# Two small groups of attention matmuls issued as pairs on halves of the TensorE array

## The chip, the cores and the metric

The kernel runs on one core of one Trainium2 chip. The metric is the device time of one execution in microseconds (us). Three runs of the kernel before gave 1731.4, 1724.58 and 1718.41 us; the median is 1724.58 us.

## The reference

Inputs: q, k, v of shape 8 x 8 x 576 x 64 (batch, heads, sequence, head size), p of shape 8 x 8 x 32 x 64, and the weights of two feed-forward blocks. All are float32.

```python
def sm_attn(qq, kk, vv):
    s = scale * np.matmul(qq, kk.transpose(0, 1, 3, 2))
    a = np.exp(s - np.max(s, axis=-1, keepdims=True))
    a = a / (np.sum(a, axis=-1, keepdims=True) + 1e-09)
    return np.matmul(a, vv)
p_packed = sm_attn(p, k, v)
x = sm_attn(q, p_packed, p_packed)          # 4608 x 512 once heads are side by side
xn = x / sqrt(mean(x * x, -1) + 1e-06) * rms_g
y = (silu(xn @ w_gate) * (xn @ w_val)) @ w_out     # inner width 1536
h = y @ w_in                                        # inner width 2048
out = np.maximum(0.01 * h, h) @ w_out2
```

The two feed-forward blocks are nearly all of the arithmetic. The attention's second output is never formed for them: `A` (the second softmax's weights) is kept, the packed values are multiplied into `w_gate` and `w_val` (tile `pw`), and `x` itself is only needed for its mean of squares.

## The kernel before, in words

Attention is done in 16 units, one for a batch and half of its heads (four heads, `u` = 0 or 1). A unit has two parts. `soft1` (lines 224 to 389) does the first softmax. Its function `packed` (line 332) makes `Pm`, the packed values of four heads as a block diagonal 128 x 256: the weights `a1T` lie 96 rows by 128 columns (four heads of 32 columns each), the values `vr` 96 rows by 256 columns (four heads of 64), and six products add up in one PSUM bank `pp`. Every head's columns of weights meet every head's values, so 128 x 256 results come out of which the four diagonal blocks of 32 x 64 are wanted; the product with `mask` on VectorE (line 344) sets the rest to zero. These products are plain float32, and the profile shows each as two passes: 96 products, 192 rows of PE.

`soft2` (line 393) does the second softmax. Its function `squares` (line 505) forms `x` for the four heads, 256 columns by 576 tokens, in four products `xp`: `x` = 0 or 1 picks two heads (two heads' `Pm` as stationary operand, 128 rows by 128 columns, of which the rows of the other two heads are zero) and `c` a half of 288 tokens. ScalarE squares what is in PSUM (line 539) and GpSimd adds the squares up (line 543, from batch 2 on); for units 0 to 5 the products are plain float32 (line 532), for units 6 to 15 each is three single-pass products of float32r halves (`mm3`, line 113: high by high, low by high, high by low). `means` (line 545) sums over the columns with a product by ones.

The rest of the PE work is `mm3` as well: `pwps` (weights times packed values), `g` and `v`, `y`, and for the second block `zh`/`h` and `zo`/`o`. Units 0 to 7 lie in the first 320 us, beside the start of the first feed-forward block; units 8 to 15 lie in a stretch from about 530 to 890 us, woven into the second block on the first half of the tokens (`zh`, `zo`).

What sets the order: the tables `S1`, `S2`, `FIRST`, `SECOND` give each function a slot in the recorded program; a list scheduler with a time model of its own then moves single instructions of each engine, taking into account when their inputs and PSUM banks come free. PE, VectorE, ScalarE, GpSimd and SyncE (the DMA queue) each run their own list in order. PSUM banks for `pp` and `xp` come from the four `y` banks (`bank`, line 205; `banks`, line 194); in the first units, from the `g` and `v` banks.

Of the kernel before, what the change touches and what calls it, by code (L numbers as in the profile page):

```python
# [30 lines left out]
FASTQ = 6  # L31
# [9 lines left out]
def pack_attention_moe_kernel(  # L41
# [14 lines left out]
    nc = tc.nc  # L56
# [6 lines left out]
    P = 128  # L63
    T = 32
    NS = S // T
    CS = NS // 2
    CH = CS * T
    KP = 96
    NJ = S // KP
# [37 lines left out]
    def mm3(ps, terms, start=True, stop=True):  # L107
        seq = [t for hi, lo in (("h", "h"), ("l", "h"), ("h", "l")) for t in [(hi, lo)]]
        n = len(terms) * 3
        i = 0  # L110
        for a, b in seq:
            for (lh, ll), (rh, rl) in terms:
                mm = nc.tensor.matmul(  # L113
                    ps,
                    lhsT=lh if a == "h" else ll,
                    rhs=rh if b == "h" else rl,
                    start=start and i == 0,
                    stop=stop and i == n - 1,
                )
                i += 1  # L120
        return mm
# [104 lines left out]
    def soft1(i):  # L226
# [105 lines left out]
        def packed():  # L332
            vr = raw.pop(("v", b, u))
            pp = bank("pp" + nm)
            for j in range(NJ):
                nc.tensor.matmul(  # L336
                    pp[:, 0, :256],
                    lhsT=st["a1T"][:, j // 3, j % 3, :],
                    rhs=vr[:, :, j, :],
                    start=j == 0,  # L340
                    stop=j == NJ - 1,
                )
            Pm = st["Pm"] = att.tile([P, 4, D], F32, tag="Pm", bufs=2, name="Pm" + nm)
            nc.vector.scalar_tensor_tensor(
                out=Pm.rearrange("p h d -> p (h d)"),
                in0=pp[:, 0, :256],
                scalar=st["rin"],
                in1=mask.rearrange("p h d -> p (h d)"),
                op0=ALU.mult,
                op1=ALU.mult,  # L350
            )
            if i + 1 < NU and i + 1 != NA:
                load_v(*divmod(i + 1, 2))
# [39 lines left out]
    def soft2(i):  # L393
# [6 lines left out]
        def tile_of(key, tag, shape):  # L400
            if key not in st:
                st[key] = att.tile(shape, F32, tag=tag, bufs=bufs[tag], name=key + nm)
            return st[key]
# [98 lines left out]
                ]  # L502
                split(AT.rearrange("p s t -> p (s t)"), *st["ATs"])

        def squares(cs, x):
            Pm = raw["P", b, u][0]
            first = u == 0 and x == 0
            early = b < SUMS
            if early:

                if first:
                    sqacc[b] = []
                if u == 0:
                    if x == 0:
                        st["sq"] = keep.tile([P, 2, 2, CH], F32, tag="atf", bufs=1, name="sq" + nm)
                    sq = st["sq"][:, x]
                else:
                    sq = att.tile([P, 2, CH], F32, tag=("sq", "sql")[x], bufs=1, name=f"sq{x}" + nm)
                sqacc[b].append(sq)
            elif first:  # L520
                sq = sqacc[b] = tile_of("sqa", "sqacc", [P, 2, CH])
            else:
                sq = att.tile([P, 2, CH], F32, tag="sq", bufs=1, name=f"sq{x}" + nm)
            for xp, cs in banks(f"xp{x}" + nm, b):
                for k_, c in enumerate(cs):
                    if i >= FASTQ:
                        ds, ts = slice(x * P, x * P + P), slice(c * CH, c * CH + CH)
                        ph, pl = st["Pm"]
                        ah, al = st["ATs"]
                        mm3(xp[:, k_, :CH], [((ph[:, ds], pl[:, ds]), (ah[:, ts], al[:, ts]))])  # L530
                        continue
                    nc.tensor.matmul(
                        xp[:, k_, :CH],
                        lhsT=Pm[:, 2 * x : 2 * x + 2, :].rearrange("p h d -> p (h d)"),
                        rhs=st["AT"][:, c * CS : (c + 1) * CS, :],
                        start=True,
                        stop=True,
                    )
                nc.scalar.activation(
                    out=sq[:, cs[0] : cs[-1] + 1], in_=xp[:, :, :CH], func=AF.Square  # L540
                )
            if not first and not early:
                side[0].tensor_tensor(out=sqacc[b], in0=sqacc[b], in1=sq, op=ALU.add)

        def means(cs):
            parts = sqacc[b]
# [851 lines left out]
```

## Time and profile before

| | before |
|---|---|
| runs, us | 1718.41, 1724.58, 1731.4 (median 1724.58) |
| span of the profiled execution, us | 1725.8 |
| PE busy | 1660.3 us, 96% of the span, 9252 instructions |
| weight loads busy | 1468.4 us, 85% |
| VectorE busy | 971.7 us, 56% |
| ScalarE busy | 693.5 us, 40% |
| GpSimd busy | 396.3 us, 23% |
| mean granted clock of TensorE | 0.986 of full speed |

The profiled execution's own time is known by its span, 1725.8 us, which is 1.2 us over the median of the three runs. A matmul's row in the trace begins when it enters the array and ends when its last result is written, so neighbours overlap; what one costs in a full stream is the distance between two starts, which I call the cadence.

### The profile page before, as it was taken

Reading aid. Unit: us, or ns where it says so; the run is one execution under the profiler, and the core shown is the slowest. Engines: PE = TensorE matmul, PEld = TensorE weight load, DVE = VectorE, ACT = ScalarE, POOL = GpSimd, SP = SyncE. Lnnn points to the kernel's source line nnn. Section 1 sums busy time; section 2 is a strip of 40 time slices with the busy share of each in tenths; the row PEclk is TensorE's granted clock in tenths of the full one; section 3 lists DMA queues with packets and bytes.
Section 4 is the critical chain, followed back from the end, with each engine's and each line's share of the span. In section 5 each row is a group of like instructions: output and inputs, shape, how many; then the busy total and the mean of one; then the engine's idle time right before and its main releaser. Section 6 shows DMA issues by size and latency. Waiting matters only on the chain.

```text
span 1725.8 us, 23867 instructions
## 1 busy us (share of the span) xinstructions
PE 1660.3 (96%) x9252; PEld 1468.4 (85%) x9252; DVE 971.7 (56%) x1636; ACT 693.5 (40%) x1218; POOL 396.3 (23%) x310
## 2 busy tenths in 40 slices
PE   7698989999999999999999999999999999999997
PEld 5587889999998888888888999999988888888885
DVE  6877887788757777666644455545542323232221
ACT  3465554564425554444434433444322223222221
POOL 2355555533311232221221112322100000000000
PEclk9889999999999999999999999999999999999998
DMA  9856666587646554642317332634063101010000
GB/s 291 235 193 189 209 205 192 191 304 260 239 152 234 181 195 146 217 156 77 101 53 267 109 122 98 233 140 155 32 245 127 49 1 48 2 46 4 18 8 25
DMA packets 83365, 247.98 MB, mean 144 GB/s; under 512 B 11444, under 2 KB 17844, under 8 KB 79156
## 3 DMA queue, kind: packets, MB, share of 16 engines
q1 hardware_dynamic: 80052, 235.96, 40.1%
q0 software_dynamic: 3200, 10.49, 2.5%
q8 instruction: 73, 1.20, 0.3%
q14 instruction: 40, 0.33, 0.1%
HBM read 174.85 MB, written 61.08 MB: 137 GB/s over the span
## 4 chain that ended last, share of the span: by engine, by line
PE 79%; DMA 9%; DVE 6%; issue 2%; ACT 2%; POOL 1%; SPq 0%; DVEq 0%; ACTq 0%; POOLq 0%
PE y L113 13%; PE h L113 13%; PE o L113 13%; PE zh L113 9%; PE zo L113 9%; PE v L113 7%; PE g L113 7%; PE pwps L113 3%; PE pp L336 2%; DMA pw<-w 2%; PE s L113 1%; DMA q<-in_q_dram 1%; DMA w<-in_moe_w_in_dram 1%; DVE cvw L692 1%; PE xp L113 1%
## 5 line engine op out<-in xcount | busy, mean ns | idle before, releaser
L113 PE MATMUL y<-hh,wo 128*128 128x288 f32 x1536 | 269.2, 298 | 4.7 <-DVE y_acc L913 2.4
L113 PEld LDWEIGHTS y<-hh,wo 128*128 128x128 f32 x1536 | 226.5, 189 | 8.0 <-DVE y_acc L913 2.7
L138 POOL TENSOR_TENSOR hl<-sg,hh 128x576 fp32r<-128x576 f32 x96 | 140.8, 1467 | 349.5 <-ACT hh L130 335.5
L113 PE MATMUL o<-w,gh 128*128 128x512 f32 x640 | 212.5, 392 | 0.0
L913 DVE TENSOR_TENSOR y_acc<-y_acc,y 128x288 f32<-128x288 f32 x320 | 142.1, 450 | 104.9 <-PE y L113 103.6
L1310 DVE TENSOR_TENSOR gf<-r,h 128x512 f32<-128x512 f32 x80 | 55.0, 688 | 248.6 <-ACT r L130 248.6
L113 PE MATMUL zo<-w,zgh 128*128 128x512 f32 x512 | 172.7, 394 | 0.0
L113 PE MATMUL y<-hl,wo 128*128 128x288 f32 x768 | 164.0, 297 | 0.0
L113 PE MATMUL h<-yh,w 128*128 128x512 f32 x640 | 162.5, 393 | 0.5 <-DVE y_acc L913 0.5
L113 PE MATMUL zh<-zyh,w 128*128 128x512 f32 x512 | 161.1, 392 | 1.7 <-DVE y_acc L913 1.7
L130 ACT ACTIVATE r<-h 128x512 f32<-128x512 f32 x80 | 47.8, 598 | 261.0 <-PE h L113 261.0
L113 PE MATMUL g<-ath,pw 128*128 128x288 f32 x768 | 141.8, 299 | 8.4 <-DMA pw<-w 6.4
L113 PEld LDWEIGHTS h<-yh,w 128*128 128x128 f32 x640 | 120.0, 188 | 28.1 <-DVE y_acc L913 0.8
L113 PEld LDWEIGHTS o<-w,gh 128*128 128x128 f32 x640 | 120.1, 188 | 27.1
L138 DVE TENSOR_TENSOR pw<-pwps,pw 64x512 fp32r<-64x512 f32 x152 | 104.1, 688 | 63.0 <-ACT pw L130 60.4
L113 PE MATMUL v<-ath,pw 128*128 128x288 f32 x768 | 138.5, 299 | 0.7 <-DVE sg L890 0.6
L130 ACT ACTIVATE hh<-sg 128x576 fp32r<-128x576 f32 x96 | 65.6, 683 | 164.8 <-DVE sg L890 160.3
L113 PEld LDWEIGHTS g<-ath,pw 128*128 128x128 f32 x768 | 117.6, 189 | 15.8 <-issue 6.1
L113 PE MATMUL o<-w,gl 128*128 128x512 f32 x320 | 125.0, 391 | 0.0
L113 PEld LDWEIGHTS y<-hl,wo 128*128 128x128 f32 x768 | 124.3, 190 | 0.1
L113 PEld LDWEIGHTS v<-ath,pw 128*128 128x128 f32 x768 | 115.7, 191 | 2.1 <-DVE sg L890 1.4
L890 DVE TENSOR_TENSOR sg<-sg,v 128x576 f32<-128x576 f32 x96 | 72.2, 752 | 72.1 <-PE v L113 66.1
(161 smaller groups left out, 3072.6 us busy)
## 6 DMA issues: line engine op xcount, KB each, us to landing
w<-w_dram SPq DMA_DIRECT2D x72, 512.0 KB
w<-w_dram SPq DMA_DIRECT2D x32, 1024.0 KB
wo<-wo_dram SPq DMA_DIRECT2D x36, 512.0 KB
w_dram<-w2s SPq DMA_DIRECT2D x32, 512.0 KB
w_dram<-w SPq DMA_DIRECT2D x24, 512.0 KB
pw<-w POOLq DMA_DIRECT2D x40, 256.0 KB, 5.4
y_dram<-y_acc SPq DMA_DIRECT2D x32, 288.0 KB
w<-in_moe_w_in_dram SPq DMA_DIRECT2D x16, 512.0 KB
```

The costliest lines, as they stand in the source:

```text
L113: mm = nc.tensor.matmul(ps, lhsT=lh if a == "h" else ll, rhs=rh if b == "h" else rl, start=start and i == 0, stop=stop and i == n - 1,)
L130: nc.scalar.activation(out=o, in_=i, func=AF.Copy, scale=scale)
L138: eng.tensor_tensor(out=o, in0=a, in1=hi.bitcast(F32), op=ALU.subtract)
L336: nc.tensor.matmul(pp[:, 0, :256], lhsT=st["a1T"][:, j // 3, j % 3, :], rhs=vr[:, :, j, :], start=j == 0, stop=j == NJ - 1,)
L692: nc.vector.scalar_tensor_tensor(out=cu, in0=low, scalar=29, in1=cu, op0=ALU.logical_shift_right, op1=ALU.bitwise_or,)
L890: nc.vector.tensor_tensor(out=hf, in0=sg, in1=vps[:, :, :CH], op=ALU.mult)
L913: pace[:] = [nc.vector.tensor_tensor(out=ya, in0=ya, in1=pv, op=ALU.add).ins]
L1310: pace[:] = [nc.vector.tensor_tensor(out=gf, in0=r, in1=ps, op=ALU.max).ins]
```

## The change

In `packed`, each of the six products becomes two: one with columns 0 to 63 of the weights (heads 0 and 1 of the unit) and their own 128 columns of values, one with columns 64 to 127 and the other two heads' values. The first writes PSUM partitions 0 to 63, the second 64 to 127, both the same 128 columns of one bank. They are given to the two halves of the array's columns (tiles of 128 rows x 64 columns). VectorE's masking reads the 128 columns twice, for 256 results as before.

In `squares`, `x` = 0 needs only rows 0 to 63 of the operands and `x` = 1 only rows 64 to 127, since the other rows of `Pm` are zero there. Each product now reads only its 64 rows, on the matching half of the array's rows (tiles of 64 rows x 128 columns). The function is called per half of the tokens (`c`) and not per `x`; within a call the products of the two `x` alternate, each `x` in a PSUM bank of its own. The number of `xp` products stays. ScalarE squares each bank alone; GpSimd's adds are cut differently, with one more per unit where `u` is 1.

```diff
             for j in range(NJ):
-                nc.tensor.matmul(
-                    pp[:, 0, :256],
-                    lhsT=st["a1T"][:, j // 3, j % 3, :],
-                    rhs=vr[:, :, j, :],
-                    start=j == 0,
-                    stop=j == NJ - 1,
-                )
+                for x in range(2):
+                    xs = slice(64 * x, 64 * x + 64)
+                    nc.tensor.matmul(
+                        pp[xs, 0, :P],
+                        lhsT=st["a1T"][:, j // 3, j % 3, xs],
+                        rhs=vr[:, 2 * x : 2 * x + 2, j, :],
+                        start=j == 0,
+                        stop=j == NJ - 1,
+                    )
...
-                out=Pm.rearrange("p h d -> p (h d)"),
-                in0=pp[:, 0, :256],
+                out=Pm.rearrange("p (x h) d -> p x (h d)", x=2),
+                in0=pp[:, :, :P].to_broadcast([P, 2, P]),
...
-        def squares(cs, x):
+        def squares(c):
...
+            parts = banks(f"xp{c}" + nm, b)
+            if len(parts) == 1:
+                xps = [(parts[0][0], x) for x in range(2)]
             else:
-                sq = att.tile([P, 2, CH], F32, tag="sq", bufs=1, name=f"sq{x}" + nm)
...
+                xps = [(parts[x][0], 0) for x in range(2)]
+            xs = [slice(64 * x, 64 * x + 64) for x in range(2)]
+            ds = [slice(x * P, x * P + P) for x in range(2)]
+            if i >= FASTQ:
+                ts = slice(c * CH, c * CH + CH)
+                ph, pl = st["Pm"]
+                ah, al = st["ATs"]
+                three = ((ph, ah), (pl, ah), (ph, al))
...
+            for n, (w, a) in enumerate(three):
+                for x, (xp, k_) in enumerate(xps):
                     nc.tensor.matmul(
                         xp[:, k_, :CH],
...
+                        lhsT=w[xs[x], ds[x]],
+                        rhs=a[xs[x], ts],
+                        start=n == 0,
+                        stop=n == len(three) - 1,
                     )
...
+            for sq, (xp, k_) in zip(sqs, xps):
+                nc.scalar.activation(out=sq, in_=xp[:, k_, :CH], func=AF.Square)
...
-            if not first and not early:
-                side[0].tensor_tensor(out=sqacc[b], in0=sqacc[b], in1=sq, op=ALU.add)
+            if not first:
+                side[0].tensor_tensor(out=acc[:, c], in0=acc[:, c], in1=sqs[1], op=ALU.add)
+            if c == 1:
+                t = st["sq"][1 if first else 0]
+                side[0].tensor_tensor(out=acc, in0=acc, in1=t, op=ALU.add)
...
-        ops += [lambda cs: squares(cs, 0), lambda cs: squares(cs, 1)]
+        ops += [lambda cs: squares(0), lambda cs: squares(1)]
```

The scheduler makes a new order from the changed program. Three places of PE's list show it. In a name such as `xp141_0` the digits are: call of `squares`, batch, unit half, and after the underscore the bank; `zh` and `zo` are the second block's products, on the whole array.

First, the second call of `squares` for unit 9 (batch 4, second half). Before:

```order
L113 MATMUL zh22_6602<-zyl23_6394,w10_4179 128x512
L113 MATMUL xp141_0_6487<-ATh41_6390,Pmh41_6386 128x288
L113 MATMUL xp141_0_6487<-ATh41_6390,Pml41_6387 128x288
L113 MATMUL xp141_0_6487<-ATl41_6391,Pmh41_6386 128x288
L113 MATMUL xp141_1_6488<-ATh41_6390,Pmh41_6386 128x288
L113 MATMUL xp141_1_6488<-ATh41_6390,Pml41_6387 128x288
L113 MATMUL xp141_1_6488<-ATl41_6391,Pmh41_6386 128x288
L113 MATMUL zo20_6645<-w20_4180,zgh20_6464 128x512
```

Of the change:

```order
L113 MATMUL zo20_6723<-w20_4238,zgl20_6541 128x512
L545 MATMUL xp141_0_6563<-ATh41_6460,Pmh41_6456 128x288
L545 MATMUL xp141_1_6564<-ATh41_6460,Pmh41_6456 128x288
L545 MATMUL xp141_0_6563<-ATh41_6460,Pml41_6457 128x288
L545 MATMUL xp141_1_6564<-ATh41_6460,Pml41_6457 128x288
L545 MATMUL xp141_0_6563<-ATl41_6461,Pmh41_6456 128x288
L545 MATMUL xp141_1_6564<-ATl41_6461,Pmh41_6456 128x288
L113 MATMUL zo20_6723<-w20_4238,zgh20_6540 128x512
```

The six stay together, and the upper and lower half of the rows alternate.

Second, the first call of `squares` for unit 6 (batch 3, first half). Before:

```order
L113 MATMUL xp030_0_2767<-ATh30_2662,Pmh30_2658 128x288
L113 MATMUL xp030_0_2767<-ATh30_2662,Pml30_2659 128x288
L113 MATMUL xp030_0_2767<-ATl30_2663,Pmh30_2658 128x288
L113 MATMUL xp030_1_2768<-ATh30_2662,Pmh30_2658 128x288
L113 MATMUL xp030_1_2768<-ATh30_2662,Pml30_2659 128x288
L113 MATMUL xp030_1_2768<-ATl30_2663,Pmh30_2658 128x288
L113 MATMUL g411_2817<-atl1_1086,pw41_2089 128x288
```

Of the change:

```order
L113 MATMUL v411_2906<-atl1_1122,pw41_2137 128x288
L545 MATMUL xp030_0_2824<-ATh30_2718,Pmh30_2714 128x288
L545 MATMUL xp030_0_2824<-ATh30_2718,Pml30_2715 128x288
L545 MATMUL xp030_0_2824<-ATl30_2719,Pmh30_2714 128x288
L113 MATMUL v411_2906<-atl1_1122,pw41_2137 128x288
L545 MATMUL xp030_1_2825<-ATh30_2718,Pmh30_2714 128x288
L545 MATMUL xp030_1_2825<-ATh30_2718,Pml30_2715 128x288
L545 MATMUL xp030_1_2825<-ATl30_2719,Pmh30_2714 128x288
```

Here the scheduler has put a product on the whole array (`v`) between the two halves, which no longer meet; at unit 11 more than a dozen whole-array products lie between them.

Third, the start of the program, units 0 to 3 (digits: call, batch, half). Before:

```order
L336 MATMUL pp10_459<-v10_327,a1T10_444 128x256 x6
L532 MATMUL xp000_438<-AT00_423,Pm00_216 128x288 x2
L532 MATMUL xp100_455<-AT00_423,Pm00_216 128x288 x2
L324 MATMUL ta11_0_482<-ident_88,e111_412 96x128 x3
L324 MATMUL ta11_1_483<-ident_88,e111_412 96x128 x3
L532 MATMUL xp001_475<-AT01_442,Pm01_325 128x288 x2
L369 MATMUL tp10_497<-ident_88,Pm10_466 128x128 x2
L532 MATMUL xp101_493<-AT01_442,Pm01_325 128x288 x2
L336 MATMUL pp11_504<-v11_468,a1T11_481 128x256 x6
```

Of the change:

```order
L338 MATMUL pp10_473<-v10_339,a1T10_457 64x128 x12
L324 MATMUL ta11_0_504<-ident_88,e111_424 96x128 x3
L324 MATMUL ta11_1_505<-ident_88,e111_424 96x128 x3
L545 MATMUL xp000_450<-AT00_435,Pm00_222 128x288 x2
L545 MATMUL xp100_468<-AT00_435,Pm00_222 128x288 x2
L545 MATMUL xp001_496<-AT01_455,Pm01_337 128x288 x2
L545 MATMUL xp101_514<-AT01_455,Pm01_337 128x288 x2
L371 MATMUL tp10_519<-ident_88,Pm10_486 128x128 x2
L338 MATMUL pp11_526<-v11_488,a1T11_503 64x128 x12
```

The transposes `ta` moved ahead of the `xp` products, of which eight now stand in one row.

Over the whole list of the change, PE goes from one shape of tile to another 123 times; before, all products have the whole array. 76 of the 123 lie at units 8 to 15 (8 runs of `pp`, 30 runs of `xp`), 35 at units 3 to 7 with `pp` of unit 4 (4 and 14 runs, two of them side by side), 12 at the start. Of the 30 runs of `xp`, 7 alternate as in the first place; the other 23 hold one half of the rows alone, in one to three products. Of the 14 runs at units 3 to 7, four hold one float32 product of each half and two hold three of the one and then three of the other; eight hold one half alone.

## Rows read from the trace of the kernel before

**Rows 1.** The page: busy time, share of the span, instructions
```profile
PE 1660.3 (96%) x9252; PEld 1468.4 (85%) x9252; DVE 971.7 (56%) x1636; ACT 693.5 (40%) x1218; POOL 396.3 (23%) x310
```

**Rows 2.** Busy time by stretch: length, us of each engine (instructions), clock, DMA share
```profile
0.00:100.00 100.00, 71.25 (x295) 55.36 (x295) 75.75 (x147) 44.02 (x78) 33.31 (x40) 0.91 0.85 248
100.00:320.00 220.00, 203.94 (x1283) 188.96 (x1284) 170.07 (x301) 115.97 (x208) 118.79 (x104) 0.96 0.64 197
530.00:890.00 360.00, 359.21 (x1724) 302.90 (x1724) 245.56 (x404) 173.73 (x323) 84.88 (x57) 1.00 0.45 145
```

**Rows 3.** Waits of PE: instruction, releaser, us in total, times, longest
```profile
PE g L113 <- DMA pw<-w: 6.4, 5, 2.7
PE pp L336 <- DVE qT L411: 5.5, 1, 5.5
```

**Rows 4.** Instructions of tile `pp`: ns min/median/max, first and last start, form
```profile
L336 PE MATMUL pp<-v,a1T x192: 377/379/767, 15.1 to 844.5; 96*128 96x256 f32 x192
L344 DVE SCALAR_TENSOR_TENSOR Pm<-pp,rin,mask x16: 465/484/484, 18.0 to 844.9; 128x256 f32<-128x256 f32 x16
```

**Rows 5.** Instructions of tiles `xp` and `ta`, same columns
```profile
L532 PE MATMUL xp<-AT,Pm x48: 403/406/849, 54.5 to 226.9; 128*128 128x288 f32 x48
L113 PE MATMUL xp<-ATh,Pmh x40: 292/294/402, 283.4 to 885.2; 128*128 128x288 f32 x40
L324 PE MATMUL ta<-ident,e x96: 270/273/421, 13.3 to 837.2; 128*96 128x128 f32 x96
```

**Rows 6.** Timeline of PE at one `pp`: start, us, engine, line, form, count
```profile
707.87 2.75 PE L336 MATMUL pp<-v,a1T 96*128 96x256 f32 x12
710.27 0.59 PE L113 MATMUL zo<-w,zgl 128*128 128x512 f32 x1
```

**Rows 7.** Timeline of PE at `xp` of unit 9, second call
```profile
626.55 0.29 PE L113 MATMUL xp<-ATh,Pmh 128*128 128x288 f32 x1
626.68 0.29 PE L113 MATMUL xp<-ATh,Pml 128*128 128x288 f32 x1
...
626.95 0.29 PE L113 MATMUL xp<-ATh,Pmh 128*128 128x288 f32 x1
...
627.35 0.39 PE L113 MATMUL zo<-w,zgh 128*128 128x512 f32 x1
```

**Rows 8.** Timeline of PE from 49 to 65 us
```profile
49.29 5.40 PE L336 MATMUL pp<-v,a1T 96*128 96x256 f32 x12 [5.46 <-DVE qT L411]
54.52 2.10 PE L532 MATMUL xp<-AT,Pm 128*128 128x288 f32 x8
56.47 0.82 PE L324 MATMUL ta<-ident,e 128*96 128x128 f32 x6
```

**Rows 9.** Chain that ended last, 47 to 62 us: start, us, what
```profile
47.84 1.39 DVE qT L411
49.29 5.40 PE pp L336 x12
54.69 1.94 PE xp L532 x8
57.28 0.97 PE xp L532 x4
58.47 0.97 PE xp L532 x4
59.45 2.59 PE pp L336 x12
```

**Rows 10.** Timeline at 15.1 us, PE started from idle: its first row
```profile
15.12 0.48 PE L336 MATMUL pp<-v,a1T 96*128 96x256 f32 x1 [0.90 <-ACT a1T L130]
```

**Rows 11.** Groups of GpSimd and of ScalarE at the squares: busy, mean ns
```profile
L543 POOL TENSOR_TENSOR sqa<-sqa,sq 128x576 f32<-128x576 f32 x18 | 26.5, 1473 | 88.9 <-ACT sq L539 88.8
L539 ACT ACTIVATE sq<-xp 128x288 f32<-128x288 f32 x40 | 15.3, 407 | 11.0 <-PE xp L113 8.0 <-PE xp L532 1.8 <-POOL sqa L543 1.3
L539 ACT ACTIVATE sq<-xp 128x576 f32<-128x576 f32 x6 | 3.9, 648 | 2.8 <-PE xp L532 2.8
```

More of the change, by code (lines that the diff above doesn't have):

```diff
@@ L503, in turn @@
                 split(AT.rearrange("p s t -> p (s t)"), *st["ATs"])
-        def squares(cs, x):
+        def squares(c):
             Pm = raw["P", b, u][0]
-            first = u == 0 and x == 0
             early = b < SUMS
[L509 to L516, printed above, removed]
-                else:
[L518 to L521, printed above, removed]
-            else:
-                sq = att.tile([P, 2, CH], F32, tag="sq", bufs=1, name=f"sq{x}" + nm)
[L524 to L531, printed above, removed]
@@ new lines, in squares @@
+            first = u == 0
+            if c == 0:
+                if early:
+                    if first:
+                        sqacc[b] = []
+                        t = keep.tile([P, 2, 2, CH], F32, tag="atf", bufs=1, name="sq" + nm)
+                        st["sq"] = [t[:, 0], t[:, 1]]
+                    else:
+                        st["sq"] = [
+                            att.tile([P, 2, CH], F32, tag=("sq", "sql")[x], bufs=1, name=f"sq{x}" + nm)
+                            for x in range(2)
+                        ]
+                    sqacc[b] += st["sq"]
+                else:
+                    if first:
+                        sqacc[b] = tile_of("sqa", "sqacc", [P, 2, CH])
+                    t = att.tile([P, 2, CH], F32, tag="sq", bufs=1, name="sqb" + nm)
+                    st["sq"] = [sqacc[b], t] if first else [t]
@@ new lines, in squares @@
+            parts = banks(f"xp{c}" + nm, b)
+            if len(parts) == 1:
+                xps = [(parts[0][0], x) for x in range(2)]
+            else:
+                xps = [(parts[x][0], 0) for x in range(2)]
[6 more added lines that the diff above has]
+                three = ((ph, ah), (pl, ah), (ph, al))
+            else:
+                ts = slice(0, CH)
+                three = ((Pm.rearrange("p h d -> p (h d)"), st["AT"][:, c * CS : (c + 1) * CS, :].rearrange("p s t -> p (s t)")),)
@@ L532, in squares @@
+            for n, (w, a) in enumerate(three):
+                for x, (xp, k_) in enumerate(xps):
                     nc.tensor.matmul(
                         xp[:, k_, :CH],
[L534 to L537, printed above, removed]
-                    )
-                nc.scalar.activation(
-                    out=sq[:, cs[0] : cs[-1] + 1], in_=xp[:, :, :CH], func=AF.Square
-                )
@@ L542, in squares @@
-            if not first and not early:
-                side[0].tensor_tensor(out=sqacc[b], in0=sqacc[b], in1=sq, op=ALU.add)
+                        lhsT=w[xs[x], ds[x]],
+                        rhs=a[xs[x], ts],
+                        start=n == 0,
+                        stop=n == len(three) - 1,
+                    )
+            if early:
+                sqs = [t[:, c] for t in st["sq"]]
+            elif first:
+                sqs = [t[:, c] for t in st["sq"]]
+            else:
+                sqs = [st["sq"][0][:, c], att.tile([P, CH], F32, tag="sqx", bufs=1, name=f"sqx{c}" + nm)]
@@ L545, in means @@
+            for sq, (xp, k_) in zip(sqs, xps):
+                nc.scalar.activation(out=sq, in_=xp[:, k_, :CH], func=AF.Square)
+            if early:
+                return
+            acc = sqacc[b]
+            if not first:
[3 more added lines that the diff above has]
+                side[0].tensor_tensor(out=acc, in0=acc, in1=t, op=ALU.add)
         def means(cs):
```

2 lines of the change are left out of this document (1 added, 1 removed).

## The prediction

> **What bounds the kernel now.** I read the page's busy times first, then the busy times by stretch, then PE's waits, then the timeline where the changed products stand. The reader is to see that PE is busy 96% of the span [rows 1], and that this is no average over unlike stages: units 8 to 15 lie in a stretch of 360 us in which PE is busy 359.21 us at a granted clock of 1.00, the higher of the two levels, 2.4 GHz [rows 2]. There every nanosecond that PE's stream gets shorter or longer ends in the time. From 100 to 320 us PE is busy 204 of 220 us; the waits that show are for weights that a DMA brings (6.4 us in five waits), so most of a gain there counts, and I count all of it. In the first 100 us PE is busy 71 us and the clock is 0.91; DMA and VectorE lead there, and a gain counts only where the chain runs through PE, which it does from 49 to 62 us [rows 2, 3, 9].
>
> **The prices of the stream as it is.** Twelve passes of `pp` take 2.75 us with the last one's 0.379 in full, so the cadence is (2.75 - 0.379) / 11 = 0.216 us and a run of twelve costs 2.59 us [rows 4, 6]. A float32r `xp` product follows the last one after 0.13 us, six cost 0.79 [rows 7]. A float32 pass of 288 columns has (2.10 - 0.406) / 7 = 0.242 us [rows 5, 8]. A float32 pass of 128 columns, the size that `pp` gets, shows only in `ta`: (0.82 - 0.273) / 5 = 0.109 us, 0.273 being one pass's own length [rows 5, 8].
>
> **What the halves can save.** No row of before has two products in the array side by side. So I bound each run: nothing, if the halves take turns; and all of the second half, if they overlap fully.
> `pp`: 24 passes of 0.109 for 12 of 0.216. Taking turns, 2.62 us, saving nothing. Fully overlapped, 1.31, saving 1.28. Between them: a product's own two passes use the same half and must follow each other, and starts stay in the order of the list. Then a pair of products takes two passes plus twice the step from one start to the next start that needs no free half. The nearest row for that step is the `zo` product whose row begins at 710.27, 0.03 us after the start of the last `pp` pass (707.87 + 2.75 - 0.38 = 710.24) [rows 6]. A pair takes 2 x 0.109 + 2 x 0.03 = 0.278, six pairs 1.67, saving 0.92 a run. I take this one, since it asks of the array only what its list says. Eight runs in the bound stretch: 7.4 us (0 to 10.2). Four at units 4 to 7: 3.7 (0 to 5.1).
> `xp`, the seven alternating runs: 3 x 0.13 + 0.03 = 0.42 for 0.79, saving 0.37 each, 2.6 us (0 to 2.7). The four runs with one float32 product of each half overlap one pass of four: 0.24 - 0.03 = 0.21 each; the two runs of three and three overlap one product, 0.10 each: 1.0 us together. The other 31 runs have no partner beside them: a product on half of the rows streams the same 288 columns, and saves nothing.
> Start: on the chain between 49 and 62 us `pp` shrinks from 5.40 (part of it at the lower clock) and 2.59 us by about a third, 1.9 and 0.9, and the eight `xp` products in a row from 3.88 to 4 x (2 x 0.242 + 2 x 0.03) = 2.18 us, 1.7 [rows 9]. Behind it the chain goes on through weights, GpSimd and a DMA, which may be late on their own account. Of 4.5 us I take half, 2.3 (0 to 4.5).
> Sum of savings: 10.0 in the bound stretch, 4.7 at units 3 to 7, 2.3 at the start: 17.0 us (0 to 23.5).
> The Trainium skill's page "TensorE: Matmul & The Clock Gate", in "Part 3: Packing small matmuls", has a pack of tiles last one matmul plus about 4 ns per further tile; by that the `pp` runs would sit near the full overlap and the sum near its upper end. No row of before can show it.
>
> **What the change of shape costs.** Before, every product has the same shape of tile, and the next one enters without a gap: an `xp` row lasts 0.294 us and its successor starts after 0.13, so 0.163 us of each product's travel lies under the next [rows 5, 7]. Now the shape changes 123 times, and about 117 of these lie where PE leads (76, 35, and 6 on the chain at the start). What one costs no row shows. Below: nothing, if each half of the array simply takes its own products. Next: the weights cannot be loaded ahead across a change; the nearest row is the `pp` pass that starts from idle, 0.48 us long against 0.379, so 0.10 us for the load that is not covered [rows 4, 10]. Next: the array must be empty first, with the weights loaded meanwhile: the 0.163 us. Above: both, 0.27 us. I take 0.163 us: a product on the whole array cannot enter rows or columns that a half product of another shape is still leaving, and the trace loads weights under the running product nearly everywhere. 117 x 0.163 = 19.1 us.
>
> **The rest.** VectorE's masking keeps its 256 columns (0.48 us) [rows 4]. ScalarE gets up to six squares of 576 columns cut in two, 2 x 0.407 for 0.648, one microsecond in all on an engine that is 40% busy [rows 1, 11]. GpSimd adds the same columns in six more pieces, which it does with 275 us idle of 360 in the bound stretch [rows 2]; if that cover were gone it would cost the fixed part of six adds, under 6 x 1.473 us, all of one add each [rows 11]. The new order also moves DMA issues and `y` products by a few places; PE's waits beyond 100 us are single ones of up to 2.7 us [rows 3], so I allow 5 us either way and count nothing.
>
> **Sum.** -17.0 + 19.1 = +2.1 us against the profiled execution's 1725.8, which is 1.2 us above the median: 1727.9 there, 1727 as the median of runs. I forecast no change that can be measured: 1% is 17 us, about what a measurement of this kernel can tell from no change.
>
> **Rivals.**
> The change of shape is free or nearly so (0 to 0.06 us). For it: the trace has the starts of unlike products 0.03 us apart [rows 6]. Against it: those were of one shape. The sum is -17 to -10, 1708 to 1715; with full overlap as well, -23.5, 1701.
> Only the weight load is exposed, 0.10 us: 117 x 0.10 = 11.7, net -5, 1719. It speaks for this that the trace loads each product's weights while the one before it is running, and that this is the part most bound to the form of the tile.
> The full stop, on the other side: the array empties and only then takes the new weights, 0.27 us at each change, in the stretch from 530 to 890 us above all (76 x 0.27 = 20.5 against 10.0 saved). The whole is 31.6 - 17.0 = +14.6, 1739. It decides against the change from 17.0 / 117 = 0.145 us a change on, and reaches 1% from 0.29 us on. The Trainium skill says on "TensorEngine Tiling (Array Packing)", under "Key Properties", that changing the mode of tiling, not just the tile, drains TensorE; that is this rival or the case I took, by whether the load waits as well, and no row of before can agree or disagree.
> The halves do not overlap for float32 (the change doesn't do what it says for `pp` and the start): only the 2.6 and 0.2 us of the float32r runs are left, and 19.1 us are paid: +16, 1741. For it: nothing in the rows shows overlap. Against: nor does anything exclude it.
>
> **How the numbers follow.** Drain alone 0.29, centre 1727; load alone 0.23, 1719; free 0.16, 1701 to 1715; full stop 0.20, 1739; no overlap 0.12, 1741. Each has 5 us around it for the order. The range 1706 to 1742 leaves out the lower end of the free case (about 0.06) and half of the dearest two (about 0.14). Faster by over 1% (under 1707) needs the free case with more than the middle overlap: 0.1. Slower by over 1% (over 1742): half of the dearest two and a little for a change dearer than 0.27: 0.2. Within 1%: 0.7.
>
> **What would show it.** In the changed kernel's timeline of 530 to 890 us: a run of `pp` from its first start to the next product's true start, 1.7 us if right, 1.3 or 2.6 for the bounds; the gap ahead of and behind such a run, 0.163 us more than the cadence if right. A lone `xp` product between `zo` products shows the price of two changes without any saving. The stretch holds the same other work, so its end moves by the sum: units 8 to 15 should end 2.4 us later (76 x 0.163 - 10.0). I am wrong if that stretch is shorter by 5 us or longer by 8, or if the first 320 us move by more than 8.

## The result and the profile after

The changed kernel takes 1748.78 us, the median of four runs (1746.3 to 1752.94), where the kernel before takes 1724.08, the median of four. The ratio is 1.0139 [1.0115, 1.0164]: slower by 1.4%. The prediction was 1727 us with a range of 1706 to 1742, so the time lies outside it, on the slow side. Times are medians of the executions of a kernel; one execution of e10, 6410 us against 1729 to 1734 for the others, counts as slow and is left out.

The profiled execution has a span of 1746.6 us, 20.8 more than before. The page of after, busy time of each engine, share of the span and instructions:

```profile
PE 1663.2 (95%) x9444; PEld 1448.3 (83%) x9444; DVE 972.4 (56%) x1636; ACT 694.6 (40%) x1224; POOL 394.8 (23%) x316
```

PE's busy time is nearly that of [rows 1]; the span grew by seven times as much. So the time did not go into longer products alone: PE idles more. Busy time by stretch, after (length, us of each engine with its instructions, granted clock, DMA share, GB/s):

```profile
0.00:100.00 100.00, 69.76 (x336) 51.83 (x337) 73.98 (x142) 41.99 (x79) 30.31 (x37) 0.86 0.83 236
100.00:320.00 220.00, 199.07 (x1305) 178.04 (x1304) 175.20 (x302) 118.67 (x209) 117.79 (x106) 0.96 0.65 203
530.00:890.00 360.00, 352.59 (x1768) 283.66 (x1767) 234.60 (x394) 168.41 (x315) 80.85 (x57) 0.99 0.46 149
```

Against [rows 2] the stretch of units 8 to 15 has lost 6.6 us of PE's busy time in 360 and a little of its clock; there the prediction had put a stream that is never interrupted. PE's waits of after from 520 us on show what is new (instruction, releaser, us in total, times, longest):

```profile
PE pp L338 <- ACT a1T L130: 5.5, 1, 5.5
PE g L113 <- DVE pw L138: 4.1, 1, 4.1
PE xp L545 <- ACT ATh L130: 1.3, 2, 0.7
```

The first two are single waits, at 813 and 955 us. Before, the longest wait from there on is one of 1.2 us.

To place the 20.8 us I cut both traces at events of the same work: the start of the first `zh` product, the start of the last `zo` product, and the first `h` of the next stage. All numbers are us, read from the traces of before and after; PE's idle time is a stage's length less PE's busy time in it.

| | before | after | difference |
|---|---|---|---|
| start to first `zh` | 508.7 | 514.0 | +5.3 |
| first `zh` to last `zo` (units 8 to 15) | 425.0 | 436.3 | +11.3 |
| last `zo` to first `h` | 337.9 | 342.0 | +4.1 |
| first `h` to end | 454.2 | 454.2 | 0 |
| PE idle in the first / second / third | 50.1 / 1.9 / 1.8 | 59.5 / 7.4 / 4.7 | +9.4 / +5.5 / +2.9 |
| at half clock in the first / second / third | 41.0 / 0 / 0 | 44.4 / 13.7 / 3.4 | +3.4 / +13.7 / +3.4 |

The middle stage, which the prediction gave +2.4 us, has +11.3. Of its 13.7 us at half clock, 10.2 begin in the wait at 813 us; the other 3.4 lie at its very start, behind the waits of the first stage.

**What a visit to a half costs, in the rows.** PE at one `pp` of units 8 to 15 in after (start, us, engine, line, form, count):

```profile
716.70 0.61 PE L113 MATMUL zh<-zyh,w 128*128 128x512 f32 x2
717.24 1.53 PE L338 MATMUL pp<-v,a1T 96*64 96x128 f32 x24
718.70 0.50 PE L113 MATMUL zh<-zyl,w 128*128 128x512 f32 x1
719.04 0.39 PE L113 MATMUL zo<-w,zgh 128*128 128x512 f32 x1
```

Twenty-four passes lie in 1.53 us, of which the last one's own length is 0.273: (1.53 - 0.273) / 23 = 0.055 us a pass, half of the 0.109 that a pass of this size takes alone [rows 5, 8]. Single starts in the trace show how: one pass of each half, 6 to 7 ns apart, and from the second pair on a new pair every 0.109 us. The halves overlap fully. The second `zh` of the first row starts at 716.92 (0.61 - 0.39 after 716.70). From there to the `zo` at 719.04 are 2.12 us, of which two `zh` take 2 x 0.23, so the run and both changes of shape took 1.66 where `pp` took 2.59 before [rows 4, 6]. Full overlap is 12 x 0.109 = 1.31, which leaves 0.35 for the two changes, 0.175 each.

A lone run of three `xp` products of one half, after:

```profile
584.48 0.39 PE L113 MATMUL zh<-zyh,w 128*128 128x512 f32 x1
584.80 0.40 PE L545 MATMUL xp<-ATh,Pmh 64*128 64x288 f32 x1
585.04 0.29 PE L545 MATMUL xp<-ATh,Pml 64*128 64x288 f32 x1
585.17 0.29 PE L545 MATMUL xp<-ATl,Pmh 64*128 64x288 f32 x1
585.39 0.50 PE L113 MATMUL zh<-zyh,w 128*128 128x512 f32 x1
585.74 0.40 PE L113 MATMUL zh<-zyl,w 128*128 128x512 f32 x1
```

From 584.48 to 585.74 are 1.26 us for two `zh` (0.46) and three products that took 0.13 each before (0.39) [rows 7]: 0.41 us too much, for nothing saved. Over the lone runs of the trace it is 0.39, so 0.195 for a change. The first row of a new shape is long by 0.11 (0.40 for 0.29, 0.50 for 0.39). The weight loads of the same moment show what goes with it:

```profile
584.26 0.19 PEld L113 LDWEIGHTS zh<-zyh,w 128*128 128x128 f32 x1
584.80 0.18 PEld L545 LDWEIGHTS xp<-ATh,Pmh 64*128 64x128 f32 x1 [0.35 <-DVE PT L359]
584.91 0.19 PEld L545 LDWEIGHTS xp<-ATh,Pml 64*128 64x128 f32 x1
585.39 0.19 PEld L113 LDWEIGHTS zh<-zyh,w 128*128 128x128 f32 x1 [0.17 <-issue]
```

The `zh` product at 584.48 had its weights loaded from 584.26, 0.22 us ahead. The first product of another shape has its load and its own row begin together, at 584.80 and at 585.39, some 0.09 us after the stream before it has ended (584.48 + 0.23 = 584.71). So at this change the load is not ahead; it starts before the `zh` row has ended at 584.48 + 0.39 = 584.87. I read the 0.11 that the first row is longer as the time until its first operand enters, which would be at 584.91, about when that row has ended; the rows do not show the operand itself.

An alternating run of six, after:

```profile
626.73 0.39 PE L113 MATMUL zo<-w,zgh 128*128 128x512 f32 x1
627.05 0.40 PE L545 MATMUL xp<-ATh,Pmh 64*128 64x288 f32 x2
627.28 0.29 PE L545 MATMUL xp<-ATh,Pml 64*128 64x288 f32 x2
627.42 0.29 PE L545 MATMUL xp<-ATl,Pmh 64*128 64x288 f32 x2
627.64 0.50 PE L113 MATMUL zo<-w,zgh 128*128 128x512 f32 x1
627.98 0.39 PE L113 MATMUL zo<-w,zgl 128*128 128x512 f32 x1
```

626.73 to 627.98 is 1.25 us, less two `zo` 0.80 us for the six: what they took before, 0.79 [rows 7]. Two products at once save 0.39 us and the two changes cost 0.39.

With these prices the stream of the middle stage is 8 x (-0.94) for `pp`, 23 x 0.39 for the lone runs and nothing for the seven alternating ones: -7.5 + 9.0 = +1.5 us, near the forecast of +2.4. The other ten microseconds are idle time and lost clock.

**The stall at 813 us.** The chain that ended last, after, 785 to 822 us (start, us, what):

```profile
791.39 9.20 DMA out_dram<-zob
800.61 0.32 SPq L1100
...
801.02 0.55 SPq L1043
...
801.67 0.54 SPq L165
802.21 0.05 issue
802.26 8.27 DMA q<-in_q_dram
...
810.62 1.39 DVE qT L413
812.03 1.16 ACT qh L130
813.19 0.38 ACT a1T L130
```

`pp` of unit 14 waits in the middle of its run for the second half of its weights `a1T`. ScalarE's list has `qh` of unit 14 between the two halves of `a1T`; `qh` waits for VectorE's `qT`, that for the load of `q`. The load stands on SyncE's queue behind four stores of output rows (`out_dram<-zob`) and three loads of `zob` that stand between them. The third of these (L1100) goes out at 800.61, as the 9.20 us of a store end (791.39 + 9.20 = 800.59); then come the fourth store and the load of `q`. The place on SyncE's list, before (first fence) and after (second):

```
L1033 DMA zyl_8446<-y_dram 128x512
L165 DMA q_7834<-in_q_dram 64x1152
L166 DMA q_7834<-in_q_dram 64x1152
L1019 DMA out_dram<-zob_7761 4x32x512
L1076 DMA zob_8299<-op_dram 128x512
```

```
L1057 DMA zyl_8558<-y_dram 128x512
L1043 DMA out_dram<-zob_7859 4x32x512
L1043 DMA out_dram<-zob_7865 4x32x512
L1043 DMA out_dram<-zob_7871 4x32x512
L1100 DMA zob_8405<-op_dram 128x512
L1100 DMA zob_8411<-op_dram 128x512
L1100 DMA zob_8428<-op_dram 128x512
L1043 DMA out_dram<-zob_7877 4x32x512
L165 DMA q_7932<-in_q_dram 64x1152
L166 DMA q_7932<-in_q_dram 64x1152
```

Before, the load stood ahead of four stores and was issued at 780.45 us; after, it stands behind them, and is issued at 801.67. What that costs PE, busy time by stretch of after:

```profile
805.00:811.00 6.00, 3.08 (x23) 2.17 (x21) 0.38 (x1) 0.00 (x0) 0.00 (x0) 1.00 0.34 110
811.00:821.00 10.00, 6.79 (x24) 4.33 (x24) 7.82 (x13) 4.27 (x7) 1.16 (x1) 0.50 0.24 70
```

The wait is 5.5 us, from 808.1 to 813.6. At 811.1, still in it, the granted clock falls to 0.50, the lower of the two levels, 1.2 GHz, and it stays there until 821.3, so that PE works at half speed for the next 7.7 us.

### The profile page after: what moved, and what is told of

Read it like the earlier page. It is cut to its first block, busy times and chain, and to the rows that moved or that the text cites. A ratio compares the mean times of both kernels' runs of the same rounds, so it can differ in the third digit from the quotient of the medians.

```text
span 1746.6 us, 24256 instructions
## 1 busy us (share of the span) xinstructions
PE 1663.2 (95%) x9444; PEld 1448.3 (83%) x9444; DVE 972.4 (56%) x1636; ACT 694.6 (40%) x1224; POOL 394.8 (23%) x316
## 4 chain that ended last, share of the span: by engine, by line
PE 72%; DMA 11%; DVE 10%; issue 3%; ACT 2%; SPq 1%; POOL 1%; DVEq 0%; ACTq 0%
PE y L113 13%; PE h L113 13%; PE o L113 13%; PE g L113 7%; PE zh L113 7%; PE v L113 7%; PE zo L113 6%; PE pwps L113 2%; DMA q<-in_q_dram 2%; DMA w<-in_moe_w_in_dram 2%; DMA w<-in_moe_w_out_dram 1%; DMA pw<-w 1%; PE xp L545 1%; DVE cvw L710 1%; PE s L113 1%
## 5 line engine op out<-in xcount | busy, mean ns | idle before, releaser
L113 PEld LDWEIGHTS y<-hh,wo 128*128 128x128 f32 x1536 | 225.7, 189 | 15.1 <-DVE y_acc L937 9.4
L113 PEld LDWEIGHTS zh<-zyh,w 128*128 128x128 f32 x512 | 96.1, 189 | 24.4 <-DVE y_acc L937 3.5
```

The costliest lines, as they stand in the source:

```text
L113: mm = nc.tensor.matmul(ps, lhsT=lh if a == "h" else ll, rhs=rh if b == "h" else rl, start=start and i == 0, stop=stop and i == n - 1,)
```

## The experiments

The first four runs separate the edits (is `pp` cut? is `squares` regrouped, and if so on half of the rows?); the other six are about the order.

**e1_pp_only.** The kernel before with the cut of `packed` alone: one array half for each pair of heads, `squares` as it was.

```diff
-                nc.tensor.matmul(pp[:, 0, :256], lhsT=..., rhs=vr[:, :, j, :])
+                for x in range(2):
+                    xs = slice(64 * x, 64 * x + 64)
+                    nc.tensor.matmul(pp[xs, 0, :P], lhsT=...[xs], rhs=vr[:, 2 * x : 2 * x + 2, j, :])
```

> Only the packed values' products (pp) are pairs on halves of the columns; the squares are as before. Theory A (the halves work as the trace of the change shows, 2.60 -> 1.66 us a run of pp with both changes of shape in it; the loss is in the lone half-row products and in the new order of the list): twelve runs behind 100 us save 0.94 us each, so 11 us less, 1713 us, give or take 6 for the order. Theory B (any change of shape costs more than the rows beside it show, for instance by weights loaded late for many products behind it): no gain, 1724 or more. Theory C (the new order alone decides, whatever the products): anything between 1715 and 1745, and PE's waits, not its stream, explain the difference.

1712.37 us, ratio 0.9909 [0.989, 0.9928]: 14.6 us faster than the kernel before, where 11 were expected, give or take 6. In the profiled execution 5.9 of it lie in the middle stage, where eight runs of `pp` at 0.94 make 7.5, and 8.6 ahead of the first `zh`, where four runs make 3.8 and the clock was at half for 10 us less than before. Its page:

```profile
PE 1644.2 (96%) x9444; PEld 1448.0 (85%) x9444; DVE 972.0 (57%) x1636; ACT 697.1 (41%) x1222; POOL 395.1 (23%) x310
```

Its stretch from 530 to 890 us:

```profile
530.00:890.00 360.00, 358.05 (x1825) 298.05 (x1824) 240.10 (x402) 170.19 (x320) 85.80 (x58) 1.00 0.46 146
```

PE does the same number of products as after in 19 us less, and the stretch has no stall. The loss sits in the other half of the change, or in the two together.

**e4_regrouped.** The kernel before with `squares` called per half of the tokens, products of the two `x` alternating, but each on all 128 rows: no change of shape at all.

```diff
-                        lhsT=w[xs[x], ds[x]],
-                        rhs=a[xs[x], ts],
+                        lhsT=w[:, ds[x]],
+                        rhs=a[:, ts],
```

> Only the grouping of the squares is changed: products, banks, squares and adds grouped by half of the tokens, all on the whole array, pp as before. No change of shape is left. Theory A and B: the order alone, 1724 to 1734. Theory C: most of the loss of the change is here, 1740 or more.

1724.14 us, 0.9983 [0.997, 0.9995]. By itself the regrouping costs nothing; ScalarE's and GpSimd's added pieces are hidden, as the prediction had it.

**e3_xp_only.** e4 with the half rows, as in the change (the diff is that of e4 read backwards).

> Only the squares are changed (regrouped, half rows); pp as before. 36 half-row runs are lone in this list, 13 have partners. Theory A: 36 x 0.39 = 14 us more than the next kernel (the same grouping on all rows), about 1740 to 1745. Theory B: far more. Theory C: the two differ by under 4 us.

1738.07 us, 1.0056 [1.0039, 1.0073]. Against e4 the half rows cost 13.9 us. The lone runs at 0.39 us, 36 of them, make 14.0. By stages the fit is looser: 23 lone runs, 9.0 us, for +7.9 in the middle stage, and 13, 5.1 us, for +7.7 ahead of the first `zh`, where the profiled execution also has 2.4 us more idle time and 10 us more at half clock. In the middle stage there is no stall; PE idles 0 us there, and units 8 to 15 are busy throughout:

```profile
530.00:890.00 360.00, 360.00 (x1690) 294.04 (x1689) 241.05 (x400) 171.81 (x319) 80.80 (x59) 1.00 0.46 149
```

So in the middle stage the half rows of `squares` are a loss of stream time, of about the price that the single rows show.

**e2_regrouped_pp.** The whole change with the same edit as in e4: `pp` cut, `squares` regrouped, on all rows.

> The change, but the squares' products use all 128 rows of the array (the rows of zeros included); grouping, banks and adds as in the change, and nearly the same order of the lists. Theory A: 31 lone half-row runs of 0.39 us each are gone, the seven alternating and two three-and-three runs stay equal, so 12 us less than the change: 1737 us; the wait of 5.5 us in the middle of a pp run near 813 us and the wait of 4.1 us near 955 us stay. Theory B: 1725, like before. Theory C: like the change, 1745 to 1750.

1730.9 us, 1.0019 [1.0006, 1.0031]. By e1 (-14.6) and e4 (-2.8) it should be about 17 us faster than the kernel before; it is 4 us slower than the one it ran beside. About 21 us appear only when both edits are made, with no kind of change of shape that e1 does not have. Against the change itself, e2 is 18 us faster, where the lone runs' price had given 12. By the stages of the table, e2 less e1 less e4 plus before:

| | to first `zh` | units 8 to 15 | last `zo` to `h` |
|---|---|---|---|
| before | 508.7 | 425.0 | 337.9 |
| e1 | 500.1 | 419.1 | 338.0 |
| e4 | 504.9 | 424.5 | 338.0 |
| e2 | 504.9 | 428.6 | 342.0 |
| of both together | +8.6 | +10.0 | +3.9 |

The last two are the stalls of after: e2 has a wait of 4.4 us at `pp` of unit 14 and one of 3.8 us at `g`, with 10.2 and 3.4 us of half clock, and e1, e3 and e4 have neither. These 14 us go with the order that the scheduler makes of the two edits together, and they are as large as the cost of the half rows in e3.

Much of the 21 us is likely clock. With the two levels 1.00 and 0.50, the mean granted clock of all executions gives an estimate of the time at half clock, (1 - clock) x 2 x span: 48 us before, 39 in e1, 39 in e4, 63 in e2. That is 33 us more than the two edits by themselves would give, which costs up to half of it, 16 us, where PE has work.

**e5_qh_behind.** Which part of the chain at 813 us counts? One theory was ScalarE: `qh` stands between two halves of `a1T`, and would only have to stand behind. The other: everything behind the late `q` waits anyway, and the stall moves on. In the change, `qh` of unit 14 is held in the order in which it is recorded, behind `a1T`.

```diff
-                    split(qT, st["qh"], st["ql"])
+                    if i == 14:
+                        ins = nc.scalar.activation(out=st["qh"], in_=qT, func=AF.Copy, scale=1.0)
+                        tc.keep_in_program_order(ins)
+                        sub(nc.vector, st["ql"], qT, st["qh"])
+                    else:
+                        split(qT, st["qh"], st["ql"])
```

> The whole change, with one instruction of ScalarE's list held back: the copy qh of unit 14's queries, which the scheduler had put between the two copies of the same unit's a1T, stays behind what was recorded ahead of it. Tiles, pairs and lone runs are nearly as in the change (121 changes of shape for 123). Theory A (the loss is lone half-row runs plus one bad place in the order, with what follows from it): the wait of 5.5 us inside unit 14's pp and the low clock behind it go, 9.5 us, and the wait near 955 us, which comes of the last unit being late, goes too, 4 us: 13 us less than the change, 1735 us, 1.006 of before. Theory D (the query transfer is late whatever waits for it): PE waits a little later instead, 1744 or more. In between, 1739: the wait near 955 us has a cause of its own.

1746.38 us, 1.0128 [1.011, 1.0147], no better than after within the intervals. `pp` no longer waits; a wait of 7.4 us stands a few products on. PE's waits from 700 to 1000 us:

```profile
PE xp L550 <- ACT ATh L130: 7.4, 1, 7.4
PE g L113 <- DVE pw L138: 4.3, 1, 4.3
```

**e7_regrouped_pp_behind.** The same hold in e2.

> Pairs for pp, regrouped squares on all 128 rows, and the same copy held back. Theory A: 13 us less than without the hold, so 1718 us, 0.995 of before, 4 to 6 us above the kernel with pp alone. Theory D: 1728 or more.

1733.28 us, 1.0047 [1.003, 1.0064]: no gain over e2 either, and a wait of 7.5 us at `xp`. ScalarE's order is not the cause; the first theory falls, and what is left is VectorE's `qT`, and behind it the load.

**e8_query_first.** The change, with the load of unit 14's `q` issued ahead of the four stores on SyncE, as it stands before. Six rows of SyncE's list differ from those of the change; the lists of the other engines are the same.

```diff
-        load_rows(t.rearrange("p s j t -> p (s j t)"), qf, b, u)
+        qload[b, u] = load_rows(t.rearrange("p s j t -> p (s j t)"), qf, b, u)
...
-                store_rows(i * 4 + t, obz[t], slice(0, DM))
+                ahead = qload[7, 0] if s_ == NZ else None
+                with tc.issue_after(ahead.ins) if ahead else nullcontext():
+                    store_rows(i * 4 + t, obz[t], slice(0, DM))
```

> The whole change, and in SyncE's list the two transfers that load unit 14's queries go back ahead of the four stores of zob40 to zob43, where they stand before the change; the lists of the other four engines are word for word those of the change. Theory E (the order lost by that one swap: the load waits behind stores, the transpose qT at the head of VectorE's list waits for the load, and PE for what is behind it): the wait of 5.5 us near 813 us, the low clock behind it and the wait of 4.1 us near 955 us all go, 13 us less than the change, 1735 us, 1.006 of before; from first zh to last zo 427 us for 436, and from there to first h 338 for 342. Theory F (the transfers are late for another reason, such as their buffer): under 4 us less.

1739.38 us, 1.0083 [1.0064, 1.0103]: 9 us less than the change. The middle stage shrinks from 436.3 to 427.5 us. The same moment in its trace, SyncE's issues:

```profile
798.22 0.47 SPq L165 DMA_DIRECT2D q<-in_q_dram  x1
798.74 0.59 SPq L166 DMA_DIRECT2D q<-in_q_dram  x1
799.38 2.55 SPq L1044 DMA_DIRECT2D out_dram<-zob  x4
```

The stretch that was disturbed in after:

```profile
811.00:821.00 10.00, 10.00 (x49) 6.84 (x44) 3.15 (x6) 2.99 (x7) 0.80 (x1) 1.00 0.51 161
```

The stall at 813 us and its slow clock are gone: the place of one load on one queue is their cause. The load is still issued 18 us later than before; it goes out 3.5 us earlier than in after, or 5.4 us counted from the first `zh`, and `qT` begins at 803.5 in place of 810.62. With this the middle stage is 2.5 us longer than before, close to the prediction's sum for it (+2.4). But I had expected the wait of `g` at 955 to go too, and it stayed at 3.7 us. So that one has a cause of its own.

**e9_regrouped_pp_query_first.** The same edit in e2.

> Pairs for pp, regrouped squares on all 128 rows, and the same swap undone. Theory E: 13 us less than without it (1731), 1718 us, 0.995 of before, as near to the kernel with pp alone (1712) as the grouping alone is to before. Theory F: 1728 or more.

1723.19 us, 0.9986 [0.9973, 0.9998], 8 us less than e2; its middle stage takes 416.9 us, 11.7 less than that of e2 and 8.1 less than that of the kernel before, about the 7.5 that eight runs of `pp` at -0.94 give. Taken against the kernel before beside each, the gain over e2 is 5 us (+4.0 to -1.3). e9 stays 11 us above e1, so the swap gives back the middle stage's part of the 21 us and not the rest: its stages ahead of the first `zh` and behind the last `zo` are 5.7 and 3.1 us longer than those of e1. The wait of `g` stays here as well, with 3.0 us.

**e6_pairs_queued.** Do the halves pay if they always meet? e5, with each product of `squares` tied behind the one of the other half, so that more runs alternate (seven of six products, six of five, three of four; in the change, seven of six).

```diff
-                for x, (xp, k_) in enumerate(xps):
-                    nc.tensor.matmul(...)
+                for x in (1, 0):
+                    xp, k_ = xps[x]
+                    with tc.issue_after(last.ins) if last else nullcontext():
+                        last = nc.tensor.matmul(...)
```

> As the first of these three, and the products of each call of the squares are recorded and queued as one chain that alternates the halves, so that fewer stand alone: at units 8 to 15 the runs of xp are 7 of six, 6 of five, 3 of four, 3 of two and 6 single products, which at 0.13 us a step and 0.39 us a visit make 16.8 us for 21.7. Theory A: 5 us less than the first of these three, 1730 us, 1.003 of before. If lone products are not what costs: no difference.

1738.9 us, 1.0084 [1.0068, 1.0099], 7.5 less than e5. Some of it is a shorter stall (3.5 us at `xp` in place of 7.4), so this one run does not give the pairs' share alone.

**e10_pairs_queued_query_first.** The same pairs in e8, where no stall at 813 disturbs the reading.

> The change with the swap undone and the products of each call of the squares queued as one alternating chain (fewer lone ones: 16.8 us of xp runs at units 8 to 15 by 0.13 us a step and 0.39 us a visit, for 21.7). Theory of the price of lone products: 5 us less than the first of these three, 1730 us, 1.003 of before. If lone products are not what costs: the same as the first.

1730.7 us, 1.0035 [1.0015, 1.0055], 8.7 less than e8, where 5 were expected; still slower than the kernel before, and 7.5 us slower than e9, which has no half rows. Tied pairs take back about half of the 16 us that the half rows cost between e9 and e8. In the profiled executions the middle stage takes 418.2 us, 9.3 less than in e8 and only 1.3 more than in e9; of the 9.3, some 2 are idle time and half clock that e8 has and e10 has not. What still parts e10 from e9 lies mostly outside the middle stage: 3.5 us ahead of the first `zh` and 4.3 behind the last `zo`.

**The wait of `g`, read from the traces.** The chain that ended last in after, 920 to 958 us:

```profile
926.96 1.36 DVE atf L613 x2
928.34 3.16 DMA at_dram<-atf
931.56 7.88 DMA atr<-at_dram
...
943.07 9.02 DMA atr<-at_dram
952.11 1.26 ACT ath L130 x2
953.39 0.60 ACT pw L130
954.01 0.71 DVE pw L138
954.85 3.16 PE g L113 x12
```

`atf`, the end of unit 15's second softmax, goes through memory and back, and the two loads take 7.9 and 9.0 us; ScalarE's `pw` stands behind the `ath` that waits for them. I take it that how early `atf` is done against the last `zo` decides. Before:

```profile
899.41 0.78 DVE L589 STREAM_TRANSPOSE atf<-A 128x576 f32<-128x576 f32 x1 [2.12 <-POOL A L588]
```

That is 34 us ahead of the last `zo`. In after, e2, e8 and e9 it is 23.4 or 23.5 us ahead, since VectorE's list has it two pairs of `zgf` and `zgl` further back; in e5 and e7 it is 24.1, with waits of 4.3 and 3.5 us. In e1, e3 and e4, which have no wait for `pw`, it is 28.4 or 28.7. But in e6 and e10 it is 15.7, and the wait of `g` is only 2.8 us, with 1.8 at `pwps` ahead of it, so this distance is not all. No run moved it alone: that this place is the cause is argued from the traces, not shown, and why the scheduler chose it stays open. So does the first stage: 8.6 us of what both edits cost together lie ahead of the first `zh`, where two kernels whose lists of PE are the same that far differ by 6 us (515.2 in e6, 509.3 in e10), and I can't put them to one cause.

## Why the prediction was wrong

**What bounds the kernel: right, and not followed.** PE's stream set the time, and an interruption of it cost more than its own length, because the clock went with it. That makes waits in this stretch dear, and the sum had them at nothing.

**The step that failed: "I allow 5 us either way and count nothing" for the new order.** e2 shows about 21 us that come with the order of the two edits together, some 10 of them in the bound stretch; moving one load gave back 9 us of that stretch in e8 and 12 in e9. What makes the other 12 or so, ahead of the first `zh` and behind the last `zo`, stays open. The rows of the order's lists were at hand: SyncE's list of the change has the load behind four stores, and before it stood ahead of them; I had not compared that queue at all, and looked at [rows 3] of before, where no late wait shows, instead of asking what stands behind a waiting instruction in the new lists. Those rows were also read short: the longest wait of before beyond 100 us is one of 3.1 us, of `xp` for `AT`, and not 2.7.

**The saving of `pp`: too low.** The prediction took 0.92 us a run, between nothing and 1.28, by two assumptions: that a product's own two passes follow each other, and that starts stay in the list's order. The first fits the trace, the second does not: the second half's first pass starts 6 to 7 ns after that of the first half, ahead of the first half's own second pass. So full overlap, 1.28, is what a run saves ahead of the changes of shape. Net of these a run saves 0.94, where the prediction had 0.92 - 2 x 0.163 = 0.59. The forecast run of 1.7 us was measured at 1.57 from its first start (717.24) to the next product's true start (719.04 - 0.23 = 718.81).

**The price of a change of shape: right in kind, a little low.** 0.163 us was the drain alone; 0.175 for column halves and 0.195 for row halves were measured. The cases "free" (0 to 0.06) and "only the load" (0.10) fall, and so does the full stop at 0.27: the load overlaps the drain, and what is measured beyond 0.163 is 0.01 to 0.03. The Trainium skill, on "TensorEngine Tiling (Array Packing)" under "Key Properties", says that changing the mode of tiling drains TensorE; this trace agrees, and the price is what this kernel adds. The full-stop rival, at 1739, came nearer to the result than the forecast, but not by its mechanism: at most 0.03 us of a change is missing from the forecast, under 4 us in 117 changes.

**`xp`: right by the pair, and the count was the loss.** Alternating runs save 0.39 us in the array, as the prediction had it (0.37), and pay 0.39 for the two changes, where it had 0.33. The lone runs, 31 with the early units, pay 0.39 for nothing. For `xp` as a whole its own terms give 44 runs at 2 x 0.163, less 3.6 saved, +11 us; e3 against e4, with 36 lone runs, gave 13.9, and e8 against e9, with 31, gave 16.2; in the middle stage the 23 lone runs account for 9.0 of 10.6 there.

**The rival that float32 halves don't overlap: wrong**, by the 24 passes of `pp` in 1.53 us. **ScalarE and GpSimd at nothing: right**, by e4.

**The sum.** The two terms of the stream, -17.0 and +19.1, were both mis-sized, both too low, and their errors cancelled: that the stream of the middle stage came to +1.5 for a forecast of +2.4 is in part luck. Of the middle stage's +11.3 us, 5.5 are idle time, and of the 13.7 us at half clock some 11 lie outside the wait at 813 and cost half their length, 5.5. The three add up to 12.5, about a microsecond more than measured. The prediction's own mark for this stretch, wrong if it is "longer by 8", was hit, and what hit it was the order and not a price.

The whole does not close as well. With e1 (-14.6), e4 (-2.8), e3 against e4 (+13.9) and the 21 us of e2, the change should be 18 us slower than before; it is 24.7, and no run places the other 7. Nor was a change of 1% the least that can be measured, as the prediction had it: the intervals here are about 0.25% either way.

## What to carry to other kernels

Two halves of the array pay when one visit holds enough work on both of them: twelve float32 passes on each half gave 1.28 us for 0.35, six float32r products broke even, and products that end up alone lose the whole visit, so cut only what an order keeps together. When a scheduler makes the order anew, compare every engine's list, the DMA queues' above all, for a load that now stands behind transfers that wait, before a sum of prices is believed. And price a wait on the engine that leads with its clock: 5.5 us idle here were followed by 7.7 us at half speed.

## What the runs showed of the hardware

Products of the two halves do not keep the list's order. At unit 6 the list has three products of one half and then three of the other:

```
L545 MATMUL xp_0_2862<-ATh_2718,Pmh_2714 128x288
L545 MATMUL xp_0_2862<-ATh_2718,Pml_2715 128x288
L545 MATMUL xp_0_2862<-ATl_2719,Pmh_2714 128x288
L545 MATMUL xp_1_2863<-ATh_2718,Pmh_2714 128x288
L545 MATMUL xp_1_2863<-ATh_2718,Pml_2715 128x288
L545 MATMUL xp_1_2863<-ATl_2719,Pmh_2714 128x288
```

The trace of after has them in pairs, the two of a pair 0.01 us apart:

```profile
288.78 0.41 PE L545 MATMUL xp<-ATh,Pmh 64*128 64x288 f32 x2
289.02 0.30 PE L545 MATMUL xp<-ATh,Pml 64*128 64x288 f32 x2
289.15 0.30 PE L545 MATMUL xp<-ATl,Pmh 64*128 64x288 f32 x2
```

The `xp` of the second half went into its half of the array at once, ahead of two products of the first half that stand before it. The Trainium skill, on "TensorE: Matmul & The Clock Gate" in "Part 3: Packing small matmuls", has matmuls start in the order of the program; for two halves of the array these rows do not agree. The same part of the Trainium skill puts the starts of a pack about 4 ns apart; here the trace agrees for the alternating float32r runs of `xp` at units 8 to 15, mostly 3 ns (0 to 5), and not for `pp`, 6 to 7 ns, or for the two runs of three and three, 10 to 12.

A visit to the halves, with its change of shape on the way in and on the way out, costs 0.35 us with halves of columns and 0.39 with halves of rows, at a granted clock of 1.00; for halves of rows the first row on the way in and the first on the way out are each long by 0.11.
